# Linear attention and eight soft-routed experts on one core: in-order weight halves, four half-contraction products, a planned PSUM set-up and a new order

## The chip, the core and the metric

The kernel runs on one core of a Trainium2 chip. The metric is device time in microseconds (us) of one execution; lower is better. Time before: 967.11 us, median of 3 runs (967.07 to 968.21).

## What is computed

The reference, cut to what matters:

```python
# attention, 8 batches x 8 heads x 576 tokens x 64
q_p, k_p = phi(q), phi(k)            # phi(x) = where(x > 0, x, exp(x) - 1) + 1
kv  = einsum('bhsd,bhse->bhde', k_p, v);  z = sum(k_p, axis=2)
x   = einsum('bhsd,bhde->bhse', q_p, kv) / (einsum('bhsd,bhd->bhs', q_p, z)[..., None] + 1e-6)
# x becomes 4608 tokens x 512; the routing weights P are 4608 x 8
P = exp(x @ w_gate - max)
for _ in range(8):                   # rows and columns are normalised in turn
    P /= P.sum(1) + 1e-9;  P /= P.sum(0) + 1e-9;  P *= N / E
out = sum over e of P[:, e] * (maximum(x @ w1[e], 0) @ w2[e])     # 512 -> 1024 -> 512
```

Every token passes through all eight experts, so nearly all the work is matrix products in 16-bit floats.

## The kernel before

**Stages.** The attention is done in 16 steps `n = 2b + g`, half the heads of one batch each (`att`, L245). A step loads k, q and v (L259), makes phi of k and q (`exp` on ScalarE at L274, two VectorE operations at L278 and L283), multiplies k with v (`kv_ps`, L310), transposes q (`qt_ps`, L337), and makes the denominator (`den_ps`, L352), the numerators (`num_ps`, L376, three pieces), their quotients (`xn`, L381, VectorE) and the transposes of those (`xt_ps`, L392, two). A copy puts each of the two into `xT`, the transposed tokens, channel block by channel block. An even step gives channel blocks 0 and 1, an odd step blocks 2 and 3.

The experts work on units of 512 tokens (`g` from 0 to 8). In expert 0 the first five units are plain: `layer1` (L534) makes eight products `hq` (`f` from 0 to 7, one for each 128 hidden features, each of four matmuls 128x512 over the four channel blocks), ScalarE applies the relu (L556), and `unit_plain` multiplies with w2 (`ye`, L773, two halves of four matmuls for each of four token tiles). All other units use seven products in place of eight for a two by two block product (`block7`, `unit`); their first ones are the rows `hq`, `att` and `Zye` of L667. In between stand the logits (`lg_ps`, L410, four groups of 36 matmuls with 8 columns) and the normalisation of P.

**PSUM.** `p_ye` names the banks of the y products: `ye0` and `ye1`, and later two banks `Zt` that take the place of the attention's `kv` bank pair. `p_hq` has two banks for `hq`, `p_att` two for all products of the attention. The numerators of the steps `n < 2` use `ye0` and `ye1` for two of their three pieces (`ps_home`, L249).

**Filling.** TensorE gets 47 matmuls `yw` on zeros (L483), of the lowest priority, so that it has work while the first inputs come.

**Loads.** `load_w` (L199) loads a weight matrix through GpSimd's DMA queue, in `parts` pieces. Those of expert 0 come in two halves each: of w1, hidden features 0 to 511 and 512 to 1023; of w2, rows 0 to 511 and 512 to 1023. A first y half (`half=0`) needs the first half of w2. The steps 2 to 5 load k, q and v through the same queue, all others through SyncE's.

**The order.** Nothing runs in the order of the source. Every operation is given to a planner (`_Plan`, L18) with a duration, what it depends on, a priority and, for some, a choice between ScalarE and VectorE. The planner then walks through time and emits the operations, and each engine executes its own in the order emitted. The numbers in `ranks` (from L991 on) replace the priority of nearly every operation, and fix some choices of engine (`:act`, `:dve`). So the engines' orders are fixed when the program is built. In the steady stage, from expert 1 on, a list (`order`) chains TensorE's products one after the other.

Of the kernel before, what the change touches and what calls it, by code (L numbers as in the profile page):

```python
# [10 lines left out]
FP32 = mybir.dt.float32  # L11
# [111 lines left out]
def kernel(  # L123
# [75 lines left out]
    def load_w(ten, nm, pl, ap, cut, e, prio, parts=1, after=0.0, deps=()):  # L199
# [6 lines left out]
        for i in range(parts):  # L206
            def fn(_, i=i):
                dst, a, off = g["tile"], [list(x) for x in ap], e * DM * F
                if parts > 1:
                    n = a[cut][1] // parts  # L210
                    off += i * n * a[cut][0]
                    a[cut][1] = n
                    dst = dst[:, i * n:(i + 1) * n, :] if cut == 1 else dst[:, :, i * n:(i + 1) * n]
                nc.gpsimd.dma_start(out=dst, in_=AP(tensor=ten.tensor, offset=off, ap=a))
            ti = add(("pool", 1.0), fn, use=[g], prio=prio, deps=[tal])
            ts_.append(add(("dma", 5.3 / parts), lambda _: None, deps=[ti], use=[g], prio=prio, lat=2.6))
            w_last[0] = ti
# [16 lines left out]
    w_last, in_prev = [None], [None]  # L234
# [10 lines left out]
    def att(b, g):  # L245
# [3 lines left out]
        def ps_home(i):  # L249
            if n < 2 and i < 2:  # L250
                return p_ye[i], yps, f"ye{i}"
            return p_att, aps, "att"
# [261 lines left out]
    def f_close(_):  # L514
# [6 lines left out]
        for i, n in enumerate(("ye2", "ye3")):  # L521
            Zt[i] = zps.tile([P, 2, 256], FP32, tag=n, name=f"Z{n}")
            nc.tensor.matmul(Zt[i].rearrange("p a b -> p (a b)"), lhsT=warm[:, 0:P], rhs=warm, start=True, stop=True)
    t_close = add(("none", 0.0), f_close, deps=front_ids, prio=0.0)

# [5 lines left out]
    def layer1(e, g):  # L531
# [9 lines left out]
        ghqs = [S_.grp(p_hq) for f in range(NFT)]  # L541
        jobs = [(f, 0, NDT) for f in range(NFT)]
        if g == 0:
            jobs = [(f, c, c + 2) for c in (0, 2) for f in range(2)] + jobs[2:]
        for f, c0, c1 in jobs:
            ghq = ghqs[f]

            def f_hq(_, f=f, ghq=ghq, c0=c0, c1=c1):
                if c0 == 0:
# [72 lines left out]
    def block7(e, g, gW, tW):  # L622
# [31 lines left out]
        def pair(gi):  # L654
# [54 lines left out]
            m1 = pm(A(1, 1, gi), B11, gX, True, tw1 + [txs, prev_hq[0], t_close], 0.0)  # L709
# [275 lines left out]
    for tt in (3, 2, 1, 0):  # L985
# [5 lines left out]
        0:9.9102 36:0.6482 38:0.6287 40:9.8766 42:9.8706 43:0.6587 44:9.8778 45:0.6446 46:0.6482 47:0.6362  # L991
        49:9.8811 50:0.647 51:9.8712 52:9.9087 54:0.6404 55:0.6488 56:0.6332 57:0.6509 58:0.6497 59:9.8862
        61:0.6368 62:0.638 63:0.6575 64:9.8811 65:0.6374 66:9.8709 67:0.6359 68:9.8682 69:0.6575
        70:0.6509:act 71:0.65 73:0.6482 75:0.6485 77:0.6392 78:0.6383 79:0.6401 80:0.6512 81:0.6404
        82:9.8799 84:0.6596 85:0.6575 86:0.6611 88:0.6506 89:0.6563:act 90:0.6395 91:0.6566 92:9.8799
        93:0.6329 95:0.6392 96:9.8817 97:0.6566 98:0.6491 99:0.6608 100:0.641 101:9.8727 102:0.641:dve
        103:9.8796 104:0.6665:act 106:0.6365 108:0.6413 110:0.6425 112:9.8727 114:0.6377 116:0.6386
        117:9.8721 118:0.6437 119:9.8727 120:0.6578 121:0.656 123:0.65:act 124:0.6446 125:0.6335:dve
        127:0.6365 128:9.8784:dve 129:9.8733 130:0.6575:act 131:0.6398 132:9.8709 134:0.6503 135:9.8733
        136:0.6365 137:9.8664 138:9.8733 139:0.6488 140:0.635 141:9.8727:act 142:0.6494 143:0.659 144:0.6557  # L1000
        146:0.6497 148:9.8718 150:0.6497 151:0.632 152:0.6404 153:9.8856 154:0.6422 155:0.6386 157:0.6596
        158:0.6365 159:0.6371:act 161:0.6443 162:0.6569:act 163:0.644 164:0.6356:dve 165:0.6452 166:0.6515
        168:0.6305 169:9.8712 170:0.6398 171:0.6359 172:0.6347 173:0.6548 174:0.6446 175:0.6533:act
        176:0.6398 177:9.8703:act 179:0.6446 181:0.6386 183:9.8937 184:0.6356 185:9.8736 187:0.6491
        189:0.6479 191:0.6455 192:9.8745 193:0.65 194:0.6488 195:9.8676 196:0.6383 198:0.6437:dve 199:0.6407
        200:0.6428:dve 202:0.644 203:9.8718:dve 204:0.6626 205:0.6515 206:0.6398 207:0.6398 209:0.6539
        210:0.6572 211:0.6506 212:0.6308 213:0.6329 214:9.8775 215:0.6524 216:0.632:dve 217:9.8715
        218:0.6605:dve 219:0.6452 221:9.8748 223:0.6455 225:0.6557 226:0.6659 227:9.8745 228:0.6647
        229:0.6515 230:9.8709 232:0.6524:act 233:0.6407 234:9.8715:dve 236:0.6674 237:0.6635:act 238:0.6362
        239:9.8808:dve 240:0.6503 241:0.641 243:0.638 244:0.6476 245:0.6395 246:0.6365 247:0.659 248:9.8709  # L1010
        249:0.6386 250:9.8739 251:0.6404 252:0.6326 253:0.6356 255:0.6428 257:0.6413 259:0.6503 260:0.6497
        261:0.6635 262:0.6647 263:0.6491 264:0.6392 266:0.6398 267:9.8802 268:0.6581:dve 270:0.6371
        271:0.6395 272:0.6443 273:0.6485:dve 274:0.6476 275:9.8727 277:0.6383 278:0.65 279:0.662 280:9.8613
        281:0.6368 282:0.6383 283:0.6587 284:0.6353:act 285:0.6464 286:9.8769 287:9.8769 289:9.8688
        291:0.6431 293:0.6509 294:9.8775 295:9.8694 296:0.6509 297:9.8817 298:0.6596 300:0.641:dve
        301:9.8646 302:0.6662:act 304:0.6365 305:0.638:act 306:0.6425 307:0.6479:dve 308:9.8793 309:0.6626
        311:0.6608 312:0.6446 313:0.6458 314:0.6545 315:0.65 316:0.647 317:0.6401 318:9.8799:dve 319:0.6365
        320:0.6659 321:9.8871 322:9.8778 323:9.8739 325:0.668 327:9.8751 329:0.6494 330:0.6371 331:0.6377
        332:0.6401 333:9.8712 334:9.873 336:9.8721:act 337:0.6365 338:9.8793:dve 340:9.8643 341:0.6617
        342:0.6497 343:9.8763 344:0.6584 345:9.8733 347:9.8802 348:9.8844 349:9.8787 350:9.8724 351:9.8742  # L1020
        352:0.6488 353:0.6398 354:9.8754:dve 355:0.6416 356:9.8745 357:0.6443 359:0.6617 361:9.8724
        363:9.8802 364:0.6515 365:0.6497 366:0.641 367:0.6428 368:9.8688 370:9.8682:act 371:0.6611
        372:9.8745 374:0.6488 375:0.6362:act 376:9.8745 377:9.8745:dve 378:0.6485 379:0.6497 381:9.873
        382:0.6599 383:9.8751 384:9.8847 385:9.8748 386:9.8799 387:9.8757 388:9.8838:act 389:0.6581
        390:9.8769:dve 391:9.8766 393:0.638 395:9.879 397:0.6377 398:0.644 399:0.6596 400:9.8736 401:9.8757
        402:9.876 404:0.6461:act 405:9.8652 406:0.6608 408:9.8727 409:9.8739 410:0.662 411:0.6704 412:0.65
        413:9.8709 415:9.8754 416:9.8754 417:0.6494 418:0.6587 419:0.6437 420:9.8742 421:0.6698 422:9.8841
        423:9.8742 424:9.8796 425:9.8685 427:0.65 429:0.6413 431:0.6485 432:0.6602 433:0.6467 434:0.6629
        435:9.8736 436:9.8862 438:0.6368:dve 439:9.8787 440:0.6638 442:9.8751 443:9.8763:act 444:9.8745
        445:0.6401:act 446:9.8739 447:9.8814 449:0.6413 450:0.6599 451:0.6449 452:0.6638 453:9.8775  # L1030
        454:0.6578 455:0.6455 456:9.8724:dve 457:0.6593 458:0.6596:act 459:9.8874 460:9.8886 461:0.6596
        463:0.6374 465:9.8733 467:9.876 468:0.6491 469:9.8601 470:0.6611 471:0.6635 472:0.6602
        474:9.8763:dve 475:0.6506 476:0.6473:act 478:9.8751 479:9.8739:dve 480:0.6563 481:0.6641 482:9.876
        483:0.6416 485:0.6524 486:0.6638 487:0.6581 488:9.8742 489:0.6398 490:9.8763 491:0.6446 492:0.6629
        493:9.873 494:9.8751 495:0.6659 497:0.6662 499:0.647 501:9.8745 502:9.8751 503:0.6515 504:9.8733
        505:0.6407 506:9.8841 508:0.6416 509:9.8715 510:9.8742:dve 512:0.6458 513:9.8769 514:0.659
        515:0.635:dve 516:0.6413 517:0.638 519:0.6602 520:9.8787 521:9.8775 522:9.8706 523:0.6629 524:0.6461
        525:9.8784 526:0.6647:act 527:0.6377 528:0.635 529:9.8802 531:0.6647 533:0.6479 535:0.6602
        536:9.8844 537:9.8796 538:0.6626 539:9.8781 540:9.885 542:9.8895:act 543:0.6395 544:0.6509
        546:0.6584 547:0.6398 548:0.638 549:9.8847 550:0.6383 551:0.6539 553:0.6536 554:9.8763 555:0.6419  # L1040
        556:9.8865 557:0.6413 558:9.8811 559:0.665 560:0.6596:dve 561:0.6452 562:0.6422:dve 563:9.882
        565:9.8742 567:0.6584 569:0.6434 570:9.8838 571:9.879 572:0.647 573:9.8724 574:9.8835 576:0.6524
        577:9.8832 578:0.6404 579:9.8721:dve 581:0.6548 582:0.6422:act 583:0.6359 584:0.6398 585:0.6356
        586:9.8712 588:0.6365 589:9.8748 590:0.6401 591:0.6413 592:0.6407 593:0.6425 594:0.6578 595:9.8925
# [106 lines left out]
```

## Time and profile before

| what | value |
|---|---|
| median of 3 runs | 967.11 us |
| profiled execution, its own time | 966.88 us |
| its span, first to last instruction | 964.8 us |
| TensorE busy | 955.7 us (99%) |
| VectorE busy | 774.2 us (80%) |
| ScalarE busy | 571.8 us (59%) |
| TensorE busy from 0 to 10, 10 to 20, 20 to 35 us | 8.67, 9.95, 12.32 us |
| TensorE busy from 35 to 135 us | 99.46 us |
| VectorE busy from 35 to 135 us | 88.01 us |
| TensorE busy from 200 to 940 us | 740.00 us |
| TensorE's last matmul ends | 960.65 us |

Busy time counts intervals in which at least one instruction is in the engine. A row of the timeline merges instructions of one kind that follow each other: its start, its length, engine, line, operands, count, and in brackets the idle time before it and what ended that. The length of a matmul row includes the time in which the last result leaves the array: one `yw` of 512 columns is 0.38 us long and four are 1.02, so that matmuls follow each other every 0.2155 us. With 128 columns they follow every 0.056 to 0.059 us, with 8 columns every 0.025.

### The profile page before, as it was taken

The page shows a single profiled execution, that of the slowest core. Times are in us where ns is not written, and L with a number is a line of the kernel's source. Part 1 is how long each engine was busy: PE and PEld are TensorE (multiplying, and loading weights), DVE is VectorE, ACT ScalarE, POOL GpSimd, SP SyncE. Part 2 cuts the span into 40 slices and gives each one's busy share as a digit, 9 for nine tenths or more (in the row PEclk, how much of TensorE's full clock was granted, in tenths as well). Part 3 has the DMA queues.
Part 4 walks back from the last instruction along what each step waited for, and adds up shares of the span by engine and source line. Part 5 has one row for each costly group of instructions (what it writes and reads, how often), then busy time and mean ns, then how long its engine had stood idle before and what let it go on. Part 6 is the DMA issues. An engine that isn't in the chain of part 4 may idle for free.

```text
span 964.8 us, 21596 instructions
## 1 busy us (share of the span) xinstructions
PE 955.7 (99%) x8833; PEld 803.8 (83%) x8833; DVE 774.2 (80%) x1535; ACT 571.8 (59%) x1033; POOL 113.6 (12%) x163
## 2 busy tenths in 40 slices
PE   9999999999999999999999999999999999999998
PEld 4556676688888888888888888888888888888886
DVE  6798879978887888878887888878887888877775
ACT  6797854865555555555555555555555555555552
POOL 4100000011111111111111111111111111111110
PEclk9999999999999999999999999999999999999999
DMA  9997962252227222362226222272226322235554
GB/s 315 339 323 281 254 186 78 44 122 77 77 78 164 77 77 78 93 148 78 78 77 138 104 77 72 72 159 71 70 76 140 99 76 78 78 100 164 164 164 111
DMA packets 46420, 121.99 MB, mean 126 GB/s; under 512 B 4208, under 2 KB 18288, under 8 KB 46320
## 3 DMA queue, kind: packets, MB, share of 16 engines
q1 hardware_dynamic: 30576, 96.22, 29.8%
q0 software_dynamic: 15344, 23.87, 12.7%
q8 instruction: 69, 1.13, 0.5%
q10 hardware_dynamic: 400, 0.52, 0.2%
q14 instruction: 31, 0.25, 0.1%
HBM read 119.69 MB, written 17.69 MB: 142 GB/s over the span
## 4 chain that ended last, share of the span: by engine, by line
PE 97%; DMA 2%; DVE 1%; issue 0%; ACT 0%; ACTq 0%
PE ye L891 33%; PE hq L667 24%; PE att L667 12%; PE ye L773 7%; PE Zye L667 6%; PE Zye L891 6%; PE hq L552 3%; DMA w<-in_moe_w_dram 1%; DMA kin<-in_k_dram 1%; PE yw L483 1%; PE num_ps L376 1%; PE xt_ps L392 1%; PE kv_ps L310 1%; PE qt_ps L337 1%; PE lg_ps L410 0%; PE den_ps L352 0%
## 5 line engine op out<-in xcount | busy, mean ns | idle before, releaser
L905 DVE SCALAR_TENSOR_TENSOR acc<-ye,P_sb,acc 128x256 f32<-128x256 f32 x620 | 267.2, 479 | 128.5 <-PE ye L891 128.1
L667 PEld LDWEIGHTS <-W 128*128 128x128 f16 x2144 | 210.1, 98 | 26.9
L891 PEld LDWEIGHTS <-S 128*128 128x128 f16 x1984 | 194.1, 98 | 22.5
L891 PE MATMUL ye<-T,S 128*128 128x256 f16 x1488 | 192.8, 273 | 0.0
L667 PEld LDWEIGHTS <-w 128*128 128x128 f16 x1608 | 157.6, 98 | 21.2 <-issue 0.5
L699 ACT ACTIVATE h<-hq 128x512 f16<-128x512 f32 x134 | 80.1, 598 | 147.5 <-PE hq L667 143.8
L915 POOL TENSOR_TENSOR acc<-acc,st 128x256 f32<-128x256 f32 x124 | 87.5, 726 | 619.8 <-ACT st L912 612.4
L891 PEld LDWEIGHTS <-h 128*128 128x128 f16 x1488 | 145.6, 98 | 16.8
L667 PE MATMUL hq<-xs,W 128*128 128x256 f16 x1008 | 151.2, 273 | 0.0
L667 PE MATMUL att<-xs,W 128*128 128x256 f16 x1008 | 151.2, 273 | 0.0
L667 PE MATMUL hq<-xs,w 128*128 128x256 f16 x1008 | 140.9, 273 | 0.3 <-DVE h L702 0.3
L696 ACT ACTIVATE h<-Zye 128x512 f16<-128x512 f32 x134 | 80.1, 598 | 40.5 <-PE Zye L667 40.2
L912 ACT ACTIVATE st<-Zye,P_sb 128x256 f32<-128x256 f32 x124 | 52.1, 471 | 78.3 <-PE Zye L891 78.3
L702 DVE CUSTOM_DVE_ANT_0 h<-att,s 128x512 f16<-128x512 f32 x126 | 86.6, 687 | 11.0 <-ACT s L686 11.0
L686 ACT COPY s<-hq 128x512 f32<-128x512 f32 x126 | 73.5, 583 | 36.2 <-PE hq L667 36.2
L864 DVE TENSOR_TENSOR S<-h 128x1024 f16<-128x1024 f16 x124 | 85.2, 687 | 11.9 <-ACT h L699 11.9
L679 ACT COPY Zye<-hq 128x512 f32<-128x512 f32 x134 | 77.9, 581 | 20.7 <-PE hq L667 20.6
L702 DVE CUSTOM_DVE_ANT_0 h<-hq,s 128x512 f16<-128x512 f32 x126 | 86.5, 687 | 0.1
L773 PE MATMUL ye<-w,h 128*128 128x512 f16 x312 | 77.2, 379 | 1.7 <-DMA w<-in_moe_w_dram 1.7
L667 PE MATMUL Zye<-xs,w 128*128 128x256 f16 x504 | 75.6, 273 | 0.0
L693 ACT COPY s<-att 128x512 f32<-128x512 f32 x126 | 74.5, 591 | 0.0
L891 PE MATMUL ye<-w,S 128*128 128x256 f16 x496 | 64.3, 273 | 0.0
(108 smaller groups left out, 946.5 us busy)
## 6 DMA issues: line engine op xcount, KB each, us to landing
xs<-xd SPq DMA_DIRECT2D x63, 896.0 KB, 4.6
w<-in_moe_w_dram POOLq DMA_DIRECT2D x14, 1024.0 KB, 11.1
out_dram<-acc SPq DMA_DIRECT2D x67, 128.0 KB, 2.4
kin<-in_k_dram SPq DMA_DIRECT2D x12, 576.0 KB, 6.2
qin<-in_q_dram SPq DMA_DIRECT2D x12, 576.0 KB, 5.7
vin<-in_v_dram SPq DMA_DIRECT2D x12, 576.0 KB, 6.3
xd<-acc SPq DMA_DIRECT2D x5, 512.0 KB, 2.7
kin<-in_k_dram POOLq DMA_DIRECT2D x4, 576.0 KB, 12.1
```

Source lines behind the costliest of these rows:

```text
L667: nc.tensor.matmul(dst[:, p, :], lhsT=lhs(p, c), rhs=rhs(c), start=(first and p == 0 and c == 0), stop=(c == 1), skip_group_check=True)
L679: nc.scalar.copy(out=Zt[1], in_=gX["tile"])
L686: nc.scalar.copy(out=gs2["tile"], in_=gX["tile"])
L693: nc.scalar.copy(out=gs5["tile"], in_=gR["tile"])
L696: nc.scalar.activation(out=hd(0, 0), in_=Zt[1], func=AF.Relu)
L699: nc.scalar.activation(out=hd(1, 0), in_=gX["tile"], func=AF.Relu)
L702: nc.vector._custom_dve(TENSOR_ADD_SAT, out=dst, in0=ps, in1=sb, s0=3.0e38, s1=0.0)
L773: nc.tensor.matmul(gy[tt]["tile"], lhsT=gh["tile"][:, f, ds(P * tt, P)], rhs=gw2["tile"][:, f, :], start=(f == 0), stop=(f == NFT - 1))
L864: nc.vector.tensor_tensor(out=Sx[:, i], in0=a0, in1=a1, op=op)
L891: nc.tensor.matmul(bank(g_)[:, s, :], lhsT=lhs(s, kk), rhs=rhs(kk), start=(new and s == 0 and kk == 0), stop=(kk == 3), skip_group_check=True)
L905: nc.vector.scalar_tensor_tensor(out=dst(), in0=bank(g_)[:, s, :], scalar=P_sb[:, gg, e:e + 1], in1=dst(), op0=ALU.mult, op1=ALU.add)
L915: nc.gpsimd.tensor_tensor(out=dst(), in0=dst(), in1=gst["tile"], op=ALU.add)
```

## The change

There are four edits and a new table of ranks.

1. `load_w`: each half of a weight matrix depends on the half issued before it, so that halves go out in order.
2. `layer1`, first unit: all of the products `f` 0 to 3 are split into two half contractions (channel blocks 0 and 1, then 2 and 3), where it was `f` 0 and 1. The products `f` 2 and 3 use the y banks `ye0` and `ye1`. In return the numerators of step `n = 1` use the two attention banks alone (`ps_home`).
3. The two matmuls that set up the banks `Zt` are an operation of the planner (`f_zt`, 0.44 on TensorE), and no longer a part of `f_close`. The first product of a `block7` unit depends on it.
4. Every rank is new: another order of everything before the chained stage.

```diff
-            ti = add(("pool", 1.0), fn, use=[g], prio=prio, deps=[tal])
+            ti = add(("pool", 1.0), fn, use=[g], prio=prio, deps=[tal, w_part.get(nm) if i else None])
+            w_part[nm] = ti
...
-            if n < 2 and i < 2:
+            if n < 1 and i < 2:
                 return p_ye[i], yps, f"ye{i}"
...
-            nc.tensor.matmul(Zt[i].rearrange("p a b -> p (a b)"), lhsT=warm[:, 0:P], rhs=warm, start=True, stop=True)
+
+    def f_zt(_):
+        for i in range(2):
+            nc.tensor.matmul(Zt[i].rearrange("p a b -> p (a b)"), lhsT=warm[:, 0:P], rhs=warm, start=True, stop=True)
     t_close = add(("none", 0.0), f_close, deps=front_ids, prio=0.0)
+    t_zt = add(("pe", 0.44), f_zt, deps=[t_close], prio=0.0)
...
-        ghqs = [S_.grp(p_hq) for f in range(NFT)]
+        ghqs = [S_.grp(p_ye[f - 2] if g == 0 and f in (2, 3) else p_hq) for f in range(NFT)]
         jobs = [(f, 0, NDT) for f in range(NFT)]
         if g == 0:
-            jobs = [(f, c, c + 2) for c in (0, 2) for f in range(2)] + jobs[2:]
+            jobs = [(f, c, c + 2) for c in (0, 2) for f in range(4)] + jobs[4:]
...
-                if c0 == 0:
+                if c0 == 0 and g == 0 and f in (2, 3):
+                    ghq["tile"] = yps.tile([P, 512], FP32, tag=f"ye{f - 2}", name="hq")
+                elif c0 == 0:
                     ghq["tile"] = hqp.tile([P, 512], FP32, tag="hq", name="hq")
...
-            m1 = pm(A(1, 1, gi), B11, gX, True, tw1 + [txs, prev_hq[0], t_close], 0.0)
+            m1 = pm(A(1, 1, gi), B11, gX, True, tw1 + [txs, prev_hq[0], t_zt], 0.0)
```

The built programs show how the engines' orders move. Both have 8833 matmuls, 47 of them `yw`. TensorE's last 7013 matmuls, from 190.9 us of the profile before on, stand in the same order. GpSimd's queue, before: both w1 halves, loads of steps 2 and 3, **second** half of w2, `wg`, **first** half of w2, steps 4 and 5. After: both w1 halves, steps 2 and 3, first half of w2, second half, `wg`, steps 4 and 5. The program after in the stretch that changes most (step number n in brackets, operations that follow each other on their engine):

```
PE   ... qt(1) kv(1) yw x2 xt(0) x2 yw x2 den(1) hq f0 blocks 0-1, num(1) third piece, yw, num(1) second, yw,
     num(1) first, yw x3, xt(1) x2, hq f1, f2, f3 blocks 0-1, hq f0, f1, f2, f3 blocks 2-3, hq f4,
     qt(2) kv(2) hq f5, den(2) hq f6, num(2) two pieces, hq f7, qt(3) first piece, kv(3), qt(3) second,
     num(2) last, ye tile 0 half 0, den(3) xt(2), ye tile 3 half 0, num(3) two pieces, ye tile 3 half 1,
     num(3) last, xt(2), ye tile 0 half 1, xt(3) x2, ye tile 1 half 0, ye tile 2 both halves,
     logits of the first 9 token tiles, ...
ACT  ... exp k(2), copy to xT, exp q(2), relu f0, f1, f2, f3, exp k(3), copy of qt(2), relu f4, exp q(3),
     relu f5, copy of v(3), relu f6, f7, kv(3) scaled, ...
DVE  ... quotients(1) x3, phi k(2), copy to xT, phi k(2), phi q(2) x2, copy of v(2), phi k(3), copy of qt(2),
     kv(2) scaled, ...
```

Ahead of the first `block7` product, before: 36 logits matmuls, the two set-up matmuls, 108 logits matmuls. After: 15 transposes `xt`, 72 logits matmuls, the two set-up matmuls, 36 logits matmuls. Of the operations that may run on either engine up to there, VectorE has 18 instead of 16 copies of `qt`, 7 instead of 6 of v, 4 instead of 2 evictions of `ye`, and 7 instead of 8 scalings of `kv`.

## The prediction

> **What bounds the kernel now.** I read the page's engine table first, then the busy time by stage, TensorE's waits, the timeline of the first 36 us, and the granted clock around the logits.
>
> ```profile
> PE 955.7 (99%) x8833; PEld 803.8 (83%) x8833; DVE 774.2 (80%) x1535; ACT 571.8 (59%) x1033; POOL 113.6 (12%) x163
> ```
>
> TensorE is the bound, and no matmul goes away: both programs have 8833. From 190.9 us on the order is the same and TensorE has no gap, so the change can only win or lose what TensorE wastes before that. Its waits from 17 to 135 us:
>
> ```profile
> PE ye L773 <- DMA w<-in_moe_w_dram: 1.7, 1, 1.7
> PE hq L552 <- ACT h L556: 1.0, 1, 1.0
> PE lg_ps L410 <- DVE xT L230: 0.3, 1, 0.3
> PE xt_ps L392 <- DVE xn L381: 0.2, 1, 0.2
> ```
>
> Each line is who waited, for what, us in total, times, longest. In the timeline the two large ones are:
>
> ```profile
> 20.47 1.46 PE L552 MATMUL hq<-xT,w 128*128 128x512 f16 x6
> 22.89 1.02 PE L552 MATMUL hq<-xT,w 128*128 128x512 f16 x4 [0.96 <-ACT h L556]
> ...
> 30.52 0.67 PE L337 MATMUL qt_ps<-ident,tq 128*128 128x128 f16 x9
> 32.85 1.02 PE L773 MATMUL ye<-w,h 128*128 128x512 f16 x4 [1.66 <-DMA w<-in_moe_w_dram]
> ```
>
> The third loss is no wait. In the answer by stages, the figure after the busy times is the granted clock:
>
> ```profile
> 30.85:34.26 3.41, 1.75 (x26) 1.15 (x23) 0.54 (x2) 1.07 (x2) 0.00 (x0) 1.00 1.03 405
> ...
> 129.83:133.25 3.42, 3.31 (x117) 3.07 (x117) 3.42 (x9) 0.46 (x2) 0.00 (x0) 1.00 0.63 218
> 133.25:136.66 3.41, 3.41 (x48) 2.66 (x45) 3.27 (x9) 1.03 (x3) 0.00 (x0) 0.50 1.02 399
> ...
> 959.27:962.68 3.41, 1.38 (x13) 0.98 (x11) 1.39 (x3) 0.00 (x0) 0.00 (x0) 1.00 0.74 203
> 962.68:964.70 2.02, 0.00 (x0) 0.00 (x0) 0.00 (x0) 0.00 (x0) 0.00 (x0) 0.50 0.15 44
> ```
>
> The clock is halved for 3.41 us after the logits (129.94 to 134.03 us), although TensorE counts as busy there: 8 columns every 0.025 us are little work.
>
> **Waits that go.** I count from start to start, since a wait also costs the drain of the last matmul. Six `hq` from 20.47 at 0.2155 end at 21.76; the next starts at 22.89: 1.13 us. It is product f 2 waiting until the relu frees one of two `hq` banks; with f 2 and 3 in the y banks it is gone. Nine transposes from 30.52 at 0.056 end at 31.02; the first `ye` starts at 32.85: 1.83 us. It waits for the first half of w2, which GpSimd issues second, at 19.15. In the new order that half takes the place of the other, issued at 15.21, which landed at 29.45 (from its issue and landing in the trace); `ye` can't start before 31, so this wait goes. What is late next is the second half, landing by 32.8 as the other did; its first user now comes at about 34.0. The quotient wait before an `xt` at 37.9 us costs 0.39 the same way, and ten `xt` from 128.95 to the first logits at 129.94 cost 0.43; 72 logits matmuls, half of them not needing the newest tokens, now cover the last copies. Sum 1.13 + 1.83 + 0.39 + 0.43 = 3.8 us.
>
> **Waits that come.** I walk the new order with the old durations and landings. The numerators of step 1 now have two banks that `den` and `xt` also use, and start with the third piece, so the first transpose needs the quotient that comes last: quotients end about 19.95 instead of 19.63, and the `hq` run starts at 20.65 instead of 20.47: +0.2. The half products don't start early: f 1 to 3 stand behind the transposes of step 1, so what they hide is the copy to `xT` (0.64). 18 `hq` take 3.9, to 24.5; `qt` and `kv` take it to 25.7, f 5 to 26.55. From here ScalarE sets the pace. After the copy (21.45) it has exp 1.16, four relus of 0.55, exp 1.17, copy 0.59, relu (to 27.1), exp 1.17, relu (to 28.85), and behind each, in order, a matmul group waits: `den` for the copy, f 6 for relu f 4, f 7 for relu f 5. TensorE waits about 0.1, 0.25 and 0.55. The first `ye` then starts at 31.3, after six more `num` matmuls than before; before it was 32.85. Up to 37 us I find 0.1 more. So +0.2 and +1.0.
>
> From 37 to 129 us the trace of before shows no wait, only 0.12 us at most changes from `kv` to another product. The new order there can't be walked by hand. From below: nothing to gain, since there is nothing to remove. From above: VectorE was busy 88.0 of the 100 us from 35 to 135; the new choices add 2 x 0.45 + 0.76 + 2 x 0.69 - 0.42 = 2.6 us to it and the stretch gets 3 us shorter, so about 6 us of room stay and it isn't the bound. I bound new waits at 3 us, as much as the old front lost, and take 0.3, one more wait like the one at 129.7.
>
> The planned set-up is the same two matmuls (0.43 us) among the logits: 0. The issue order on GpSimd moves `wg` behind a half of 0.75 us; the logits need it near 39 us, it landed at 29.66: 0. If that cover were gone it would cost that landing's lateness. The first w2 half of expert 1 is issued ahead of its w1 at 111 us, wanted from 190: 0.
>
> **The clock.** In the half-clock stretch eight `hq` take 134.03 to 135.69 (1.66 instead of 0.87), four `att` 0.85 instead of 0.44, the rest 0.06: 1.26 us lost; the logits themselves keep 0.025. Does it come again? Counting columns at 0.42 ns, the 3.41 us before the drop had 24% of full work, those before the drop at the end 34%, and 30.85 to 34.26, where TensorE stood for 1.66 us, 42% with no drop. So the threshold lies between 34 and 42%. The new low stretch is 108 logits matmuls and two set-up matmuls, 3.13 us instead of 4.03. On the clock's grid (133.25 less multiples of 3.413) it lies near 128.0 to 131.2, cut by the boundary at 129.83. If the 15 transposes ahead of it (0.84 us) count as work, the two windows have about 60 and 65%: no drop. The Trainium skill, "TensorE: Matmul & The Clock Gate", Part 4, says that a transpose doesn't count as busy in the way other matmuls do: then the first has about 37%, between the two ends. Part 1 of that page adds that the window runs free of the kernel's start, so that the grid may lie elsewhere: the low stretch then fills a window enough in roughly 20 to 40% of positions. The rows can't decide the transposes (no window rests on them alone). By the rows the sum wins 1.26, by the rule 0 or, if the drop hits matmuls alone, -0.4. I take the rows, which put the cut in the middle, at about two to one.
>
> **Sum.** 3.8 - 0.2 - 1.0 - 0.3 + 1.26 = 3.5 us. The profiled execution took 966.88 us (span 964.8 and 2.1 around it), 963.4 after; the median of the runs is 0.23 above the profile, so the forecast is 963.6.
>
> **Rivals.** 0.2% (1.9 us) is about what a measurement of this kernel can tell from no change.
> - The clock drops again: 963.6 + 1.26 to 1.7 = about 965.0. For it: the rule on transposes; against: the grid.
> - The front's gain is given back, because in-order engines with 6 us of room make TensorE wait elsewhere between 37 and 190 us: 2 to 3.3 us of new waits, 966.2. For it: every rank is new, and my walk finds 1.0 us of new waits in 16 us of it; against: before, 99.46 of 100 us were busy there with the same planner.
> - Slower: VectorE becomes the bound between 35 and 135 us. TensorE must lose more than 3.5 us to be slower at all, 5.4 to show it: VectorE's work would have to grow by 6 + 5.4, 11 us, or 13%, where I count 2.6. Price at that point 969.1.
> - The change doesn't do what it says: the half products indeed start no earlier. It costs nothing in the sum, since the bank wait goes all the same; were that wait to stay as well, 963.6 + 1.13 = 964.7, inside the range (chance 0.05, counted in the first case).
>
> **Chances.** 963.6 with waits gone and clock whole 0.57 (962.2 to 964.8); clock drop 0.25 (964.0 to 966.0; two thirds of it under 965.2); gain given back 0.13 (965.2 to 968); slower 0.05. Faster by over 0.2% (under 965.2): 0.55 + 0.17 + 0.02 = 0.74, slower 0.05, the same 0.21. The range, 961.9 to 966.3, takes in the first two cases and half of the third; its low end is the first case without new waits.
>
> **What would show it.** TensorE's waits: no `ye` waiting for `w`, no `hq` waiting 1.0 for the relu near 22; instead small waits of `den` and `hq` for ScalarE near 26 to 29 us; first `ye` at 31.3; the first half of w2 landing at 29.5. The granted clock: 1.00 from 7 to 960 us. Last matmul at 957.1. It is wrong if waits stand between 37 and 190 us, or a 0.50 after the logits.

## The result and the profile after

In one comparison on the same chip the kernel after took 964.05 us (median of 6 runs, 963.61 to 965.14), the kernel before 967.32 (6 runs, 967.07 to 968.34). The ratio is 0.9966, 95% interval 0.9953 to 0.9979. The profiled execution of after took 964.13 us, its span 962.1. A repeat gave 964.76 (12 runs) against 967.13 (41 runs), ratio 0.9978 (0.9970 to 0.9987). So the change makes the kernel 2.4 to 3.3 us faster by these two comparisons; the forecast was 3.5.

The engine table of after: TensorE is busy 0.6 us less than before, VectorE 2.3 more.

```profile
PE 955.1 (99%) x8833; PEld 804.2 (84%) x8833; DVE 776.5 (81%) x1539; ACT 569.2 (59%) x1030; POOL 113.7 (12%) x163
```

TensorE's waits in the whole span (who, for what, us in total, times, longest). The line of the `yw` matmuls is the wait for their zeros at the start, which both kernels have.

```profile
PE yw L484 <- DVE warm L472: 1.3, 1, 1.3
PE hq L559 <- ACT h L563: 0.4, 2, 0.2
PE hq L674 <- DVE h L709: 0.3, 1, 0.3
PE xt_ps L393 <- DVE xT L231: 0.3, 1, 0.3
PE xt_ps L393 <- DVE xn L382: 0.2, 1, 0.2
```

Both large waits of before are gone: `ye` no longer waits for `w` (1.7), and the `hq` line for the relu (1.0 at one place) now has two waits of 0.2, one at 28.0 us, one at 105.6. The wait of the logits for the last copy (0.3) became one of the last `xt` for its bank (0.3). In the timeline of TensorE:

```profile
19.75 4.26 PE L559 MATMUL hq<-xT,w 128*128 128x512 f16 x18
...
26.47 1.02 PE L559 MATMUL hq<-xT,w 128*128 128x512 f16 x4
27.33 0.51 PE L377 MATMUL num_ps<-kvz,qpT 128*128 128x128 f16 x6
28.00 1.02 PE L559 MATMUL hq<-xT,w 128*128 128x512 f16 x4 [0.17 <-ACT h L563]
...
30.33 1.02 PE L780 MATMUL ye<-w,h 128*128 128x512 f16 x4
```

Eighteen `hq` now follow each other where six ran before the stall (4.09 us from the first to the next product, 0.21 more than 18 at 0.2155), and the first `ye` starts at 30.33 with no wait, 2.5 us earlier than before. The first half of w2 landed at 29.46.

The windows of the granted clock (in each row the figure after the five engines' busy times) show the other case of the forecast, not the one that its sum took:

```profile
126.97:130.38 3.41, 3.12 (x92) 2.64 (x89) 2.83 (x7) 1.42 (x4) 0.00 (x0) 1.00 0.39 80
130.39:133.80 3.41, 3.41 (x48) 2.66 (x46) 3.34 (x9) 0.80 (x2) 0.00 (x0) 0.50 1.05 400
```

The clock still drops behind the logits. In before's trace the drop stood at 133.25 us, here at 130.39: 2.86 us lie between, no multiple of 3.41, so the windows' boundaries are not where they were. The start of the full clock shows the same. At first one `yw` follows the other every 0.427 us, half the later speed (the figure in the rows reads 1.00 there too); by the trace's clock records that ends at 6.96 us in before's trace, at 4.09 in after's. From there to the drop it is 126.3 us in both, 37 windows of 3.413.

**Counting the drops.** Each run lists the mean granted clock of its span. One window of 3.41 us at half clock lowers the mean by 0.5 x 3.41 / 962 = 0.0018, two by 0.0035; the half clock after the last matmul costs up to about 0.001 more. So a mean of 1.000 or 0.999 is an execution without a drop, 0.998 or 0.997 one with one dropped window, 0.996 or 0.995 one with two. In all 14 traces of this study the number of windows at 0.50 between the start and the last matmul agrees with that. Sorted so, with all executions of before whose clock is listed (145) and of after (18):

| kernel | no drop | one window | two windows | median of all |
|---|---|---|---|---|
| before | 965.55 (36) | 967.06 (77) | 968.16 (32) | 967.01 |
| after | 963.80 (6) | 964.94 (12) | none | 964.68 |

This table is the key to the case: much of the spread of the times is the clock (one drop costs 1.51 us before, 1.14 after), and kernels can be compared at an equal number of drops. There the change wins 1.75 us without a drop and 2.12 with one. The runs were made on several chips; before without a drop has its median between 965.53 and 965.57 on each of the four whose clock is listed.

### The profile page after: what moved, and what is told of

The parts are those of the page before. It is cut to its first block, busy times and chain, and to the rows that moved or that the text cites. A ratio compares the mean times of both kernels' runs of the same rounds, so it can differ in the third digit from the quotient of the medians.

```text
span 962.1 us, 21598 instructions
## 1 busy us (share of the span) xinstructions
PE 955.1 (99%) x8833; PEld 804.2 (84%) x8833; DVE 776.5 (81%) x1539; ACT 569.2 (59%) x1030; POOL 113.7 (12%) x163
## 3 DMA queue, kind: packets, MB, share of 16 engines
q8 instruction: 69, 1.13, 0.5%
## 4 chain that ended last, share of the span: by engine, by line
PE 94%; DMA 2%; ACT 2%; DVE 1%; issue 0%; SPq 0%; ACTq 0%; DVEq 0%
PE ye L898 34%; PE hq L674 24%; PE att L674 12%; PE ye L780 7%; PE Zye L674 6%; PE Zye L898 6%; PE hq L559 3%; DMA kin<-in_k_dram 1%; PE kv_ps L311 1%; PE num_ps L377 1%; PE xt_ps L393 1%; PE qt_ps L338 1%; DMA qin<-in_q_dram 1%; ACT h L563 0%; PE lg_ps L411 0%; ACT ek L275 0%
## 5 line engine op out<-in xcount | busy, mean ns | idle before, releaser
L912 DVE SCALAR_TENSOR_TENSOR acc<-ye,P_sb,acc 128x256 f32<-128x256 f32 x620 | 267.2, 479 | 128.0 <-PE ye L898 127.5
L898 PE MATMUL Zye<-w,h 128*128 128x256 f16 x496 | 64.3, 273 | 0.0
## 6 DMA issues: line engine op xcount, KB each, us to landing
out_dram<-acc SPq DMA_DIRECT2D x67, 128.0 KB, 2.4
```

The source lines that it names most:

```text
L898: nc.tensor.matmul(bank(g_)[:, s, :], lhsT=lhs(s, kk), rhs=rhs(kk), start=(new and s == 0 and kk == 0), stop=(kk == 3), skip_group_check=True)
L912: nc.vector.scalar_tensor_tensor(out=dst(), in0=bank(g_)[:, s, :], scalar=P_sb[:, gg, e:e + 1], in1=dst(), op0=ALU.mult, op1=ALU.add)
```

## Experiments

In all of them the order in which the planner emitted its operations is written out as a list and kept, so that only the named edit differs. The order's own diff is given in words where a list of operations moves.

**1 to 3. The two edits alone, in the old order.** First the order of the halves:

```diff
 # GpSimd's queue in the kernel before
-... w2 half 1, wg, w2 half 0, steps 4 and 5
+... w2 half 0, wg, w2 half 1, steps 4 and 5
```

> The kernel before, with the two w2 halves of expert 0 exchanged in GpSimd's queue and every engine's order otherwise as it was. If the wait for w2 is what it cost: the first half lands near 29.5 us, the first ye starts at 31.0 instead of 32.85, and the time falls by 1.8 us, to about 965.5. If TensorE only meets the next late thing (second half, quotients, inputs of step 4): less than 0.7 us of it stays, 966.6 or more.

Second, the y banks for the products f 2 and 3, which stay whole:

```diff
-        ghqs = [S_.grp(p_hq) for f in range(NFT)]
+        ghqs = [S_.grp(p_ye[f - 2] if g == 0 and f in (2, 3) else p_hq) for f in range(NFT)]
...
+                if c0 == 0 and g == 0 and f in (2, 3):
+                    ghq["tile"] = yps.tile([P, 512], FP32, tag=f"ye{f - 2}", name="hq")
```

> The kernel before, with products hq f 2 and f 3 of the first unit in the y banks, order and all else as it was (they stay whole). If each wait counts by itself: 1.1 us faster, 966.2. If the waits stand in series: f 2 starts 1.1 us earlier, but the transposes of q(2) behind it wait for VectorE until 23.2, 0.55 us of the gain are left there, and the first ye still waits for w2 until 32.8, so the gain is 0 to 0.2 us, 967.2.

Third, both:

> The kernel before with both edits of e1 and e2, order otherwise as it was. If the waits add up: 2.9 us faster, 964.4. In series: 1.8 plus 0.55, 2.3 us faster, 965.0. The rest of the change's 3.3 us is then the new order's (1.0 us) or that of the clock's grid.

Measured: halves in order 965.71 (21 runs), ratio 0.9984 (0.9978 to 0.9991), and 1.1 us at no drop (964.43), 1.0 at one (966.05). y banks 967.15 (13 runs), ratio 1.0003 (0.9995 to 1.0011): nothing. Both 965.47 (22 runs), ratio 0.9987 (0.9981 to 0.9994), 964.24 at no drop and 965.45 at one: 0.2 and 0.6 better than the halves alone.

Why do the banks bring nothing, although they take a wait of 1.0 away? TensorE's waits with the y banks alone:

```profile
PE hq L569 <- DVE xT L245: 1.4, 1, 1.4
...
PE ye L790 <- DMA w<-in_moe_w_dram: 1.1, 1, 1.1
```

and in the timeline:

```profile
19.48 0.59 PE L569 MATMUL hq<-xT,w 128*128 128x512 f16 x2
21.48 0.38 PE L569 MATMUL hq<-xT,w 128*128 128x512 f16 x1 [1.40 <-DVE xT L245]
22.10 1.67 PE L569 MATMUL hq<-xT,w 128*128 128x512 f16 x7 [0.25 <-ACT xT L243]
...
30.72 0.95 PE L352 MATMUL qt_ps<-ident,tq 128*128 128x128 f16 x9
32.82 1.02 PE L790 MATMUL ye<-w,h 128*128 128x512 f16 x4 [1.15 <-DMA w<-in_moe_w_dram]
```

The waits stand in a row. The relu's wait is gone; in its place the products wait for VectorE's copy to `xT`, which stands behind phi of k of step 2 on that engine, and that load landed at 20.27 us here, at 18.87 in before's trace. So part of this wait belongs to the execution: the trace of the halves alone, with the load at 20.34, waits 0.7 for the copy and 0.7 for the relu. How long the copy is waited for with the load at 18.87 and the y banks, no trace shows. Behind it the first `ye` waits for the same w2 half, which lands when it lands: `ye` starts at 32.82, as before. What is won ahead of a landing that stays where it is, is taken back there. With the halves in order, no trace shows a wait for `w`, and `ye` starts at 31.85 (halves alone) and 31.07 (both).

**4. The changed kernel with the halves exchanged.**

```diff
-            ti = add(("pool", 1.0), fn, use=[g], prio=prio, deps=[tal, w_part.get(nm) if i else None])
+            ti = add(("pool", 1.0), fn, use=[g], prio=prio, deps=[tal])
...
 # GpSimd's queue in the kernel after
-... w2 half 0, w2 half 1, wg, steps 4 and 5
+... w2 half 1, w2 half 0, wg, steps 4 and 5
```

> The kernel after, with the two w2 halves of expert 0 exchanged again in GpSimd's queue, all else as it is. The first ye needs the half that is issued second and lands at 32.05: it starts at 32.1 instead of 30.33, 1.75 us slower than the kernel after, 965.8. If the new order has slack after it, as later waits of 0.2 to 0.4 us take some of it up: 1.3 us slower, 965.3. If the halves' order has nothing to do with the gain: 964.0.

966.99 (13 runs), ratio 1.0001 (0.9993 to 1.0009): by the median the whole gain is gone; at equal drops 1.4 of 1.75 us go at no drop (965.22) and 2.1 of 2.1 at one (967.00). One line is back among TensorE's waits:

```profile
PE ye L795 <- DMA w<-in_moe_w_dram: 1.7, 1, 1.7
```

The first `ye` starts at 32.79. Without the new issue order of the two halves the rest of the change brings 0.3 us at most.

**5. The changed kernel again**, with its order written out.

> The kernel after, every engine's order the same, timed beside the other kernels of this call. 3.3 us faster than before, as in its first runs, with a spread of 1.5 us between executions. If the first result was luck with the clock's grid: 2 us or less.

964.76 (12 runs), as told above, 2.4 us faster than before and so between the two cases; its executions are pooled with the first 6 in the table. Its trace is one without a drop, although all 8833 matmuls stand in the order of after's. Its full clock begins at 6.50 us, and windows of 3.413 counted from there have these rows around the logits:

```profile
125.96:129.37 3.41, 3.12 (x59) 2.41 (x58) 2.27 (x6) 1.20 (x2) 0.00 (x0) 1.00 0.06 10
129.37:132.79 3.42, 3.42 (x95) 3.06 (x92) 3.42 (x8) 1.10 (x4) 0.00 (x0) 1.00 0.86 304
```

The boundary at 129.37 cuts the logits, which run from 128.56 to 131.69, so that each window has dense products with its part of them. Counted in columns at 0.42 ns, the two windows hold 0.58 and 0.54 of full work; the window ahead of the drop in after's trace, with the logits from 127.98 on, holds 0.31. Its last matmul ends at 957.37; in the first trace of after, with a drop, at 958.11.

**6. Both edits, complete, in the old order**: the halves in order and four half-contraction products, the products otherwise where they were.

```diff
-            if n < 2 and i < 2:
+            if n < 1 and i < 2:
...
-            jobs = [(f, c, c + 2) for c in (0, 2) for f in range(2)] + jobs[2:]
+            jobs = [(f, c, c + 2) for c in (0, 2) for f in range(4)] + jobs[4:]
```

> The kernel before with the halves of w2 in order and the whole of edit 2 (four half products ahead of the copies to xT, f 2 and 3 in the y banks, numerators of step 1 in the attention banks), the old order otherwise. e3 had the banks without the splitting and still waited 0.8 and 0.25 us for the copies to xT behind f 0 and 1. If the half products are the cover for these copies: about 0.9 us better than e3, 2.2 us faster than before, 964.8. If they bring nothing because the next wait takes it: as e3, 1.3 to 1.5 us faster, 965.6, and all the rest of the change's gain is the new order's.

965.66 (13 runs), ratio 0.9990 (0.9981 to 0.9998), at one window 965.65 where experiment 3 had 965.45: splitting f 2 and 3 adds nothing in the old order. Beside the halves alone (966.05) the whole of edit 2 is worth 0.4 us there, and the kernel after, with the new order and the planned set-up, lies 0.7 below this one. The set-up (edit 3) was not tested alone.

**7. The changed kernel with the half products undone**: f 2 and 3 whole and in the `hq` banks, in the new order.

```diff
-        ghqs = [S_.grp(p_ye[f - 2] if g == 0 and f in (2, 3) else p_hq) for f in range(NFT)]
+        ghqs = [S_.grp(p_hq) for f in range(NFT)]
...
-            jobs = [(f, c, c + 2) for c in (0, 2) for f in range(4)] + jobs[4:]
+            jobs = [(f, c, c + 2) for c in (0, 2) for f in range(2)] + jobs[2:]
```

> The kernel after with the splitting and the banks of edit 2 undone for f 2 and 3 (whole products in the two hq banks, behind f 0 and 1), all else in the new order. If edit 2 is needed there: f 0 waits for the copies to xT until 21.4 us and f 2 for the relu of f 0 until about 23.0, so f 4 ends near 25.6 instead of 23.8, and the time is 1.5 to 1.8 us above the kernel after, 965.6. If the new order alone makes the gain: within 0.4 us of the kernel after.

966.05 (21 runs), ratio 0.9986 (0.9980 to 0.9993); 964.85 at no drop, 966.16 at one, so 1.05 to 1.2 us slower than the kernel after. The timeline shows the covers that are missing:

```profile
19.85 0.59 PE L572 MATMUL hq<-xT,w 128*128 128x512 f16 x2
21.18 0.38 PE L572 MATMUL hq<-xT,w 128*128 128x512 f16 x1 [0.73 <-DVE xT L246]
21.80 0.81 PE L572 MATMUL hq<-xT,w 128*128 128x512 f16 x3 [0.24 <-ACT xT L244]
23.35 2.75 PE L572 MATMUL hq<-xT,w 128*128 128x512 f16 x12 [0.74 <-ACT h L576]
```

Two copies and one relu are waited for, 2.2 us from start to start, where the eighteen of after lose 0.21 (its row at 19.75). So banks and splitting together are worth nothing with the late half of w2 (the banks in experiment 2), 0.4 us in the old order with the halves exchanged (experiment 6), and 1.05 to 1.2 in the new order. Why the new order makes more of them was not tested.

**8. Fewer filling matmuls**: 39 `yw` instead of 47, because 26 of them stand ahead of the first transposes and run at half clock for the first 4 to 7 us.

```diff
-        twa = add(("pe", 0.3), lambda e, n=2 if 4 <= i < 17 else 1: f_warm(e, n), deps=[twa], use=[gyw], prio=900.0, after=1.2 + 0.5 * i)
+        twa = add(("pe", 0.3), lambda e, n=2 if 4 <= i < 9 else 1: f_warm(e, n), deps=[twa], use=[gyw], prio=900.0, after=1.2 + 0.5 * i)
```

> The kernel after with 39 instead of 47 matmuls on zeros: 20 instead of 26 stand ahead of the first transposes. In the traces so far the first transposes start between 8.46 and 9.71 us, later the longer the clock stays at half at the start (full from 4.1 to 7.0 us), because the fillers stand ahead of them in order. If that shifts the whole kernel: first transposes near 8.4 in every execution, 0.5 us faster than the kernel after in the median and a narrower spread. If the first loads set the front anyway: no difference, within 0.2 us. If the clock then comes later or falls: slower by up to 1 us.

964.23 (6 runs), ratio 0.9969 (0.9957 to 0.9980). That looks 0.5 better than experiment 5, but at no drop it has 963.71 (4 runs) against 963.80: what differs is how many of its 6 runs had a drop. What the fillers cost does not show at the end: in this trace the first transposes wait 0.57 us instead, and start at 8.74 (8.46 in after's trace, 9.49 in that of experiment 5).

**9. Do transposes count as work for the clock?** The prediction left that open. The last five transposes are written 27 times, in a version of the kernel in which only 36 logits matmuls follow them:

```diff
-                for i in range(5):
+                for i in list(range(5)) * (27 if (b, g, c2) == (7, 1, 1) else 1):
```

> The kernel after with two of its four logits groups moved to the middle of the front (near 83 and 112 us), so that one group of 36 logits matmuls is left in the low stretch, and with the last five transposes written 27 times into the same bank instead of once: 130 more transposes of 0.056 us, a stretch of 7.5 us of transposes alone, longer than two windows of 3.41 us, so that one window holds nothing else. If a transpose counts as work like any matmul, the granted clock stays 1.00 through the stretch and the time is about 7.3 us above that of the kernel with the logits moved (some 971). If it does not count, as the rule says, that window is empty, the clock is 0.50 within or right after the transposes for at least 3.4 us, the transposes behind the drop take 0.11 us each, and the time is 972.5 to 974.

975.35 us (one run). The windows, on the grid that this trace's own drop gives:

```profile
82.89:86.30 3.41, 1.73 (x51) 1.50 (x46) 3.41 (x7) 2.26 (x4) 0.00 (x0) 1.00 0.57 162
86.30:89.72 3.42, 3.42 (x23) 1.42 (x21) 0.28 (x1) 0.82 (x2) 0.00 (x0) 0.50 1.02 393
134.09:137.50 3.41, 3.41 (x65) 3.41 (x63) 0.00 (x0) 0.00 (x0) 0.00 (x0) 1.00 0.00 0
137.50:140.91 3.41, 3.41 (x60) 3.17 (x58) 0.28 (x1) 0.00 (x0) 0.00 (x0) 1.00 0.03 5
```

From 134.09 to 137.50 TensorE does nothing but transposes, 0.056 us each, and the clock stays 1.00 there and in the window behind it. So these transposes count as work, against the rule that the prediction weighed. The total is no test, since it lies higher than either case expected: the kernel without the added transposes turned out slower than assumed (experiment 10), and there is one drop, but elsewhere. It follows a wait of 1.7 us and 36 logits near 85 us, which experiment 10 explains.

**10 and 11. The logits spread.** Two of the four groups of 36 logits matmuls moved to the middle of the front.

```diff
 # TensorE's order in the kernel after; lg(n), n from 0 to 3, are the logits of 9 token tiles
+... qt(10), lg(1), ye ...
+... qt(14), lg(2), den(14) ...
-... xt(15), lg(1), lg(3), set-up of Zt, lg(2), first block7 products
+... xt(15), set-up of Zt, lg(3), first block7 products
```

> The kernel after with two of its four logits groups moved up to where their rows of x are ready (near 83 and 112 us), each among products of the experts; the work is the same. The low stretch near 129 us shrinks from 3.1 us to about 1.4 (36 logits matmuls and the two set-up matmuls), less than half a window wherever the grid lies. If the spread of the executions of the kernel after is mainly the clock drop behind the logits (1.3 to 1.7 us, in part of them), no execution has it here: clock 1.00 at 130 us in the trace, all times within about 1 us of each other, and 0.7 to 1.2 us under the kernel after, about 963.6. If the spread comes from the length of the low clock at the start, the interval stays as wide as that of the kernel after (2 us) and the time is the same, 964.7.

> The same with 39 instead of 47 of the filler matmuls at the start. If low clock at the start and the drop behind the logits are separate losses, their gains add: 0.5 under the kernel with the logits spread, about 963.1, the fastest so far. If only one of the two sets the spread, it is the same as the better of the two alone.

966.97 (13 runs), ratio 1.0005 (0.9997 to 1.0013), and with fewer fillers 967.50 (22 runs), ratio 1.0008 (1.0001 to 1.0015). Both expectations fail: at no drop 966.65, 2.85 us slower than the kernel after. The first waits of its trace:

```profile
PE lg_ps L426 <- DVE xT L246: 1.7, 1, 1.7
...
PE att L689 <- DVE W L853: 1.1, 1, 1.1
PE hq L689 <- DVE h L724: 1.0, 2, 0.7
```

I placed one group too early (1.7 us for a copy of its tokens). The second line is the lesson: without 72 logits matmuls near 130 us the next products wait 1.1 us for `W`, the sums of weights that VectorE makes after its last copy to `xT`. The logits in one piece can cost a drop, but they cover VectorE. Four of the 13 runs still had a dropped window (11 of the 22 with fewer fillers); the trace of experiment 9, with the same front, has its drop at 86.30, behind the wait of 1.7.

**12. The logits mixed with dense products, in place.**

```diff
 # TensorE's order; hq are the first eight products of block7, which read only xT and w
-... ye, xt, xt, xt, lg(1), lg(3), set-up of Zt, lg(2), hq x4, hq x4, att ...
+... ye, lg(1), xt, xt, xt, set-up of Zt, hq x4, lg(3), hq x4, lg(2), att ...
```

> The kernel after with the same 108 logits and two set-up matmuls near 129 us, but mixed with full-width work instead of in one piece: one group of 36 stands ahead of the last 15 transposes, and between the other two stand the set-up and eight products (hq from xT and w) that came after them. The order of VectorE's and GpSimd's work is unchanged and nothing leaves the stretch, so VectorE's preparation of W keeps its cover, which it lost in the run with the logits spread. Every window of 3.41 us in the stretch now holds about 50% of full column work or more; so far the clock dropped at up to 0.40 and held from 0.42 up. If the drop behind the logits causes the upper half of the spread of the kernel after, no execution has one: clock 1.00 at 130 us, the upper end of the times about 964.3 instead of 965.3, the median 963.5 to 964. If the drop isn't what spreads the times, the median and the upper end stay at about 964.5 and 965.3. If a wait of 0.5 us or more comes where the groups stand now (the logits for the last copies, or the products for a bank), the gain is given back, and the waits of TensorE near 130 us show it.

In the code the first of these products also no longer waits for the sums `xst`, which it does not read.

964.03 (6 runs, 963.42 to 964.52), ratio 0.9971 (0.9959 to 0.9983). None of the 6 runs had a dropped window, where 12 of 18 of the kernel after had one; were the chance still two in three, six without a drop would come once in 729 times. At no drop its median is 0.24 above that of the kernel after (964.04 against 963.80, 6 runs each, which overlap). The timeline has one new wait:

```profile
129.46 1.05 PE L426 MATMUL lg_ps<-wg_sb,xT 128*128 128x8 f16 x36
130.36 0.60 PE L689 MATMUL hq<-xT,w 128*128 128x256 f16 x4
130.79 1.04 PE L426 MATMUL lg_ps<-wg_sb,xT 128*128 128x8 f16 x36
132.12 0.60 PE L689 MATMUL att<-xst,W 128*128 128x256 f16 x4 [0.28 <-ACT P_sb L430]
```

The last group stands directly ahead of a product that needs its bank, so that this product waits for the exp. Over all executions the mean is 963.94 against 964.53 for the kernel after (18 runs). It beats the kernel before by 2.7 us; that it beats the kernel after too is likely from the mean, but the two ratios to before overlap.

## Why the prediction was right, and where not

The forecast was 963.6 us, the first median 964.05, inside the range. Step by step:

- **The bound.** Right. From 190 us on nothing moved (from the first to the last of those 7013 matmuls 769.4 us before, 769.5 after), and what was won lies in front of it.
- **The wait for w2 goes (1.83).** Right. It is absent after, and exchanging the halves brings 1.7 of it back (experiment 4) and takes 1.4 to 2.1 us. The landing was forecast at 29.5 and measured at 29.46.
- **The bank wait goes (1.13).** The size is right in the new order (1.05 to 1.2, experiment 7, banks and splitting together). That it would go "all the same", whatever the half products do, is wrong: in the old order the y banks alone bring nothing, since the copy to `xT` takes the relu's place and w2's landing takes the rest. What the half products hide is that copy, as the prediction said; it did not say how late that copy can be.
- **Waits that come in the front (0.2 + 1.0).** The start of the `hq` run was forecast at 20.65; it is 20.64 in experiment 5 and 19.75 in the first trace, whose full clock began 2.4 us earlier. From there to the first `ye` the forecast was 10.65 us with 0.9 of waits; measured 9.92 and 10.58. In experiment 5 only f 7 waits, 0.14; in the first trace, where the load of k(2) landed at 19.61 and not at 18.94, the waits are 0.17 in the `hq` run, 0.26 (f 6) and 0.33 (f 7). The step that was too high is ScalarE's time: the walk laid its operations end to end by their lengths, but in before's rows too each starts about 0.1 us ahead of the end of the one before. First two rows of before, then two of experiment 5, where relu f 4 ends at 26.66 (forecast 27.1) and relu f 5 at 28.19 (28.85):

```profile
24.74 1.17 ACT L274 ACTIVATE ek<-kin 128x1152 f16<-128x1152 f32 x1
25.80 1.09 ACT L556 ACTIVATE h<-hq 128x512 f16<-128x512 f32 x2
...
26.01 0.65 ACT L578 ACTIVATE h<-hq 128x512 f16<-128x512 f32 x1
...
27.55 0.64 ACT L578 ACTIVATE h<-hq 128x512 f16<-128x512 f32 x1
```

- **Waits that come later (0.3).** Too low. Counted from start to start, as the prediction counts, the rows of experiment 5 have 0.43 ahead of 104.90, 0.40 ahead of 106.44, and 0.43 and 0.18 ahead of 128.10 and 128.56: 1.44 us. The first trace has the last three, 1.0 us. So the 0.43 ahead of the logits went, but all of it came back ahead of the last `xt`. Waits between 37 and 190 us were one of the prediction's own signs of being wrong.

```profile
103.91 0.72 PE L408 MATMUL xt_ps<-ident,xn 128*128 128x128 f16 x10
104.90 1.02 PE L574 MATMUL hq<-xT,w 128*128 128x512 f16 x4 [0.27 <-ACT h L578]
105.76 0.44 PE L408 MATMUL xt_ps<-ident,xn 128*128 128x128 f16 x5
106.44 1.02 PE L574 MATMUL hq<-xT,w 128*128 128x512 f16 x4 [0.24 <-ACT h L578]
...
127.11 0.72 PE L408 MATMUL xt_ps<-ident,xn 128*128 128x128 f16 x10
128.10 0.44 PE L408 MATMUL xt_ps<-ident,xn 128*128 128x128 f16 x5 [0.27 <-DVE xT L246]
128.56 1.94 PE L426 MATMUL lg_ps<-wg_sb,xT 128*128 128x8 f16 x72
```

- **Sum of the waits.** Forecast 3.8 - 1.5 = 2.3 us; measured at equal drops 1.75 (none) and 2.12 (one). It came near because two errors offset each other: in experiment 5 the front's waits are 0.76 smaller than forecast and the later ones 1.14 larger, which leaves 1.9.
- **The clock (1.26).** This step failed. "On the clock's grid (133.25 less multiples of 3.413) it lies near 128.0 to 131.2, cut by the boundary at 129.83" took the grid of one execution for that of the next. Full clock begins anywhere from 4.0 to 7.3 us in the 14 traces, and in the nine that have a drop it comes a whole number of windows later (24, 37 or 38 times 3.413 us): the windows run free of the kernel's start, as the Trainium skill says ("TensorE: Matmul & The Clock Gate", Part 1). The prediction named that and set it aside. The drop came back in 12 of 18 executions, more often than the 20 to 40% of positions that it counted, and a 0.50 after the logits was one of its own signs of being wrong. What did change is that the two-window drop, 32 of 145 executions before, was not seen after. With the medians of the table, after's shares of drops are worth 0.4 us on the mean, a third of the 1.26.

The other half of that step, whether transposes count, was decided as the prediction took it (experiment 9). So the forecast without a drop, 963.6, stands beside 963.80 measured, and the first rival, "the clock drops again" at 965.0, beside 964.94. Both happen, by turns; the prediction should have given a mixture of the two and not one of them. That the first median came so near to 963.6 is luck: three of its six executions had no drop, against three of the next twelve (964.76).

The rival of a gain given back came in part: no wait between 37 and 104 us, but 1.0 to 1.44 us of waits from there to the logits, against 0.43 before, where the rival asked 2 to 3.3 of new ones. VectorE as the bound did not come: its busy time grew by 2.3 us, forecast 2.6.

Open: what exactly decides on a drop. The prediction put the threshold between 34 and 42% of full work. Counted in columns, the windows at full clock ahead of the drops (those at the kernel's end left out) had 0.23 to 0.40, but three windows in that range were followed by no drop: 0.38 in the traces of experiments 1 and 3, and 0.30 in that of experiment 7. So the share of columns alone does not sort them.

## What to carry to other kernels

Waits ahead of a landing stand in a row: find the landing that comes last and move its issue first. The wait ahead of it brought nothing when removed alone, 0.4 us once the landing was early, and 1.1 in the new order. When walking an order by hand, count from start to start and not by lengths, on every engine. Compare kernels at an equal number of clock drops, and where an execution can fall on either side, forecast two times with their shares. Before moving matmuls of few columns away, ask which engine's preparation they cover; mixed with dense products in place they kept the cover, and none of six executions had a drop.

## What was not expected of the hardware

- The drop has a length: 3.41 us in eight of the nine traces that have one, but by the mean clock about one of five executions of before lost two windows. In the trace of experiment 6 the half clock lasts 6.83 us from 131.43, and its execution took 967.01 us against a median of 965.65 with one window.
- A landing moves by more than the waits that were counted: the load of step 2's k landed between 18.87 and 20.44 us in the 14 traces, with the issue order unchanged.
- 7.7 us of transposes alone keep the clock at 1.00; 108 logits matmuls of 8 columns in 3 us do not always.
